# Attention into expert-choice layer on one core: ninth-block evictions one place later, finished logits on GpSimd, row transposes in eight-tile units over two pairs of banks, and the last pair's products in one run

## The chip, the core and the metric

The program runs on one core of a Trainium2 chip. The core has TensorE (matrix products and transposes, PE in the rows; its weight loads are PEld), VectorE (DVE), ScalarE (ACT), GpSimd (POOL) and SyncE, whose queue issues most transfers (SPq). Each engine works through its own list in order; semaphores hold an instruction back until what it needs is there. PSUM, where TensorE writes, has eight banks of 128 x 512 floats. The metric is device time of one execution, in microseconds (us).

## The reference, cut to what matters

```
scores = q @ k^T / 8                       # 8 batches x 8 heads, 576 x 576, head size 64
keep   = scores >= max(row) - tau          # tau = 0.02
attn   = exp(scores - max), dropped entries 0, divided by the row sum
x      = (attn @ v), heads side by side    # 4608 tokens x 512
logits = x @ w_gate                        # 8 experts
# all 36864 logits in falling order: a token goes to the expert of its highest
# logit that still has room; an expert takes 576 tokens
out[token] = relu(x[token] @ w1[e]) @ w2[e]   # 512 -> 1024 -> 512
```

## The kernel before, in words

**Attention.** Two heads make a pair: 32 pairs, four per batch. A row tile is 128 queries by 576 keys, laid out as 128 x 2 x 288 in a pair of PSUM banks, a tile `sc` (there are two such pairs, for two heads). A pair has four and a half tiles per head, so two pairs together make nine units: a *cycle* `c` is nine passes of the loop over `s_` (I call a pass a *slot*; unit `u=s_%9`; `u==4` is the tile shared by both pairs, 64 queries of each). There are 16 cycles; two cycles are a batch.

In a slot the work of three units overlaps. `score` writes two `sc` tiles on TensorE. `mx` has VectorE copy each into SBUF as `z`, scaled, with the row minimum (`z` L87); GpSimd adds the threshold (`nb` L88); ScalarE takes the exponential (`ex`, `pp` L95); VectorE drops what is below the threshold and sums (`stt`, `pp` L98). Then TensorE transposes `pp` in blocks of 64 keys: eight of the nine blocks go into one PSUM pair `tb` (`tr`, L108), which ScalarE evicts into `pt` (`trev`, L120 for `u==4`, L123 for others). The *ninth blocks* of one or two units have no room there and are put into the spare columns (288 and up) of the second `sc` tile of the next slot (`left`, at `u` in 1, 3, 4, 6, 8); `leftev` evicts them (L136, L139). `columns` multiplies the finished `pt` by `v` (`group`, L154), accumulating over nine blocks `k` in the PSUM pair `vb`, by a table `plan` of which blocks of which pair go in which slot; `shut` (L158) evicts the sum into `xt`, the batch's transposed output.

**Logits of a batch.** After its last pair, `finish(b)` queues two steps, which run at `s_%9==5`, one per cycle. In a cycle of even number `lg_unit` (L177) multiplies `xt` by `w_gate` into `vb`, evicted as `lt`. In the next, of odd number, `lgt_unit` transposes `lt` back into `vb`, and `lgt_ev` (L195 to L200) multiplies by the reciprocal row sums and adds over the heads on VectorE, into `Lg`.

**Rows.** The experts gather token rows, so `xt` is transposed into row form and written to DRAM (`xrows`). Batches 0 and 1 do so within the loop (`rows_turn`, `rows_ev`: four 128-wide transposes in spare columns of the slot's two `sc` tiles, at `s_%9` in 3, 6, 8). The other six do so after the loop in 30 late units (`late_unit`; four transposes L221, or two L217 for the last 64 queries of a batch) through the two halves of `vb`. ScalarE evicts each (L223, L219). `rows_out` issues one 260 KB transfer per 128 rows; `short_out` (L209) issues 16 of 8 KB for the short tile.

**Router and experts.** `R.phase` searches, for one expert at a time, for the logit that 576 tokens reach: seven rounds of a comparison on VectorE (`cmp`), a count on TensorE (L457, L463, L479) and a step. For the first expert these rounds are interleaved with the late units by planned costs: each late unit is put down at `XTY` = 1.05 us, each round by its VectorE work. Then come the final threshold (`lo`), the expert's number (`e`), the token numbers (`idx`), the gather (L723), and the first product of the expert layer (L804). From there two lines of products, L804 and L836, run to the end; later experts' searches lie beneath them.

Of the kernel before, what the change touches and what calls it, by code (L numbers as in the profile page):

```python
# [18 lines left out]
S=576; D=64; HS=288; QK=2*HS+2*S; NB=9; XE=8*HS+256  # L19
PPB=8; LTB=1; VTB=4; HOLD=1; XW=520; NBO=2; NDEF=4; XTB=4; XTY=1.05; XT0=2.0; XRB=2  # L20


# [943 lines left out]
```

## Time and profile before

| | |
|---|---|
| median of 3 runs | 1026.44 us (1025.98 to 1026.49) |
| profiled execution | 1027.05 us |
| its span, first to last instruction | 1025.3 us |
| TensorE, VectorE, ScalarE, GpSimd busy | 93%, 75%, 61%, 22% |
| attention loop up to the first late unit | 0 to 467.7 us |
| late units and first search | 467.7 to 513.2 us |
| up to the first product of the expert layer | 545.6 us |
| expert layer | 545.6 to 1025.3 us |

The profiled execution's own time is 1.75 us longer than its span. The shares are averages over stages with different limits, so the stages are read one by one. TensorE's granted clock is a share of its full 2.4 GHz; 0.50 is 1.2 GHz.

### The profile page before, as it was taken

How to read it: one execution, taken by the hardware profiler on the slowest of the kernel's cores; microseconds unless marked ns; L12 is line 12 of the kernel's file. 1: busy time of each engine (PE TensorE's matmuls, PEld its weight loads, DVE VectorE, ACT ScalarE, POOL GpSimd, SP SyncE). 2: the span in 40 equal slices, each digit the busy share in tenths (PEclk: the TensorE clock that was granted, in tenths of full speed). 3: DMA queues.
4: the chain of work that ended last, by engine and by line, in shares of the span. 5: the costliest groups of instructions: out<-in, count | busy, mean ns of one | idle time of the engine just before them, and what ended most of it. 6: DMA issues, size and time to landing. Idle time of an engine off the chain costs nothing.

```text
span 1025.3 us, 25919 instructions
## 1 busy us (share of the span) xinstructions
PE 956.2 (93%) x10337; PEld 727.7 (71%) x10337; DVE 770.3 (75%) x2100; ACT 621.1 (61%) x1059; POOL 229.8 (22%) x308
## 2 busy tenths in 40 slices
PE   7999999999999999996737999999999999999996
PEld 4666666666666565664537879798897989899895
DVE  7999999999999999982237988868678787625230
ACT  6888898989889898963315435344342544535340
POOL 2222222324222322210010040313222213220201
PEclk9999999999999999997567999999999999999999
DMA  5222232523322230205244252534343416252101
GB/s 195 83 93 83 73 135 90 183 68 103 137 93 84 76 107 20 94 2 193 98 142 163 94 161 93 155 109 145 119 130 104 142 55 187 81 168 68 42 11 41
DMA packets 44312, 108.16 MB, mean 105 GB/s; under 512 B 13344, under 2 KB 14112, under 8 KB 43680
## 3 DMA queue, kind: packets, MB, share of 16 engines
q1 hardware_dynamic: 36800, 83.89, 24.2%
q0 software_dynamic: 5888, 19.03, 6.0%
q10 hardware_dynamic: 1504, 3.59, 1.1%
q8 instruction: 81, 1.33, 0.5%
q14 instruction: 39, 0.32, 0.1%
HBM read 83.77 MB, written 21.64 MB: 103 GB/s over the span
## 4 chain that ended last, share of the span: by engine, by line
PE 71%; DVE 10%; ACT 8%; issue 6%; DMA 2%; SPq 2%; ACTq 0%; POOLq 0%; POOL 0%; DVEq 0%
PE pf L804 21%; PE pf L836 19%; PE vb L154 10%; PE sc L79 8%; PE tb L108 5%; DVE pp L98 4%; DVE z L87 4%; ACT pp L95 3%; PE vb L221 2%; PE pt L749 2%; SPq L209 1%; ACT pp L223 1%; ACT xt L158 1%; PE rps L457 1%; ACT pt L120 1%
## 5 line engine op out<-in xcount | busy, mean ns | idle before, releaser
L95 ACT ACTIVATE pp<-z,nb 128x576 f32<-128x576 f32 x288 | 216.3, 776 | 50.7 <-DVE z L87 48.6
L87 DVE TENSOR_SCALAR_CACHE_REDUCE z<-sc 128x576 f32<-128x576 f32 x288 | 209.9, 750 | 23.2 <-ACT pt L139 9.8
L98 DVE SCALAR_TENSOR_TENSOR pp<-z,nb,pp 128x576 f32<-128x576 f32 x288 | 223.3, 811 | 0.1
L836 PE MATMUL pf<-w2h,H 128*128 128x512 f32 x576 | 195.6, 402 | 0.5 <-DVE H L385 0.5
L79 PE MATMUL sc<-qk 64*128 64x288 f32 (+1 forms) x1280 | 177.1, 425 | 3.5 <-ACT xr L270 2.0
L88 POOL TENSOR_SCALAR nb<-nb,taub 128x2 f32<-128x2 f32 x144 | 107.7, 748 | 309.3 <-DVE z L87 201.0
L154 PE MATMUL vb<-pt,vt 64*64 64x288 f32 (+2 forms) x2336 | 170.8, 410 | 6.4 <-DVE lwm L199 2.4
L108 PEld LDWEIGHTS tb<-ident,pp 64*128 64x128 f32 x2304 | 83.7, 139 | 71.3 <-issue 37.7
L123 ACT ACTIVATE pt<-tb 128x1024 f32<-128x1024 f32 x128 | 129.2, 1010 | 3.5 <-PE tb L108 2.4
L836 PE MATMUL pf<-w2l,H 128*128 128x512 f32 x320 | 128.4, 401 | 0.0
L154 PEld LDWEIGHTS vb<-pt,vt 64*64 64x64 f32 x2336 | 78.2, 132 | 61.8 <-issue 10.4
L836 PEld LDWEIGHTS pf<-w2h,H 128*128 128x128 f32 x576 | 106.9, 189 | 19.6 <-DVE H L385 0.9
L843 POOL DMA_INDIRECT out_dram<-y,idx x40 | 46.5, 1163 | 314.2 <-ACT y L839 203.9
L79 PEld LDWEIGHTS sc<-qk 64*128 64x128 f32 (+1 forms) x1280 | 97.1, 180 | 27.1 <-DVE z L87 7.7
L108 PE MATMUL tb<-ident,pp 64*128 64x64 f32 x2304 | 103.2, 230 | 10.3 <-ACT pt L120 4.3
L804 PE MATMUL pf<-xh,w1h 128*128 128x288 f32 (+2 forms) x512 | 110.6, 302 | 0.7 <-ACT xh L750 0.7
L804 PE MATMUL pf<-xl,w1h 128*128 128x288 f32 (+2 forms) x512 | 110.0, 301 | 0.0
L804 PE MATMUL pf<-xh,w1l 128*128 128x288 f32 (+2 forms) x512 | 110.0, 301 | 0.0
L839 ACT ACTIVATE y<-pf 128x512 f32<-128x512 f32 x40 | 23.9, 597 | 125.9 <-PE pf L836 119.5
L816 ACT ACTIVATE hf<-pf 128x576 f32<-128x576 f32 x56 | 36.5, 651 | 90.0 <-PE pf L804 83.4
L804 PEld LDWEIGHTS pf<-xh,w1h 128*128 128x128 f32 x512 | 82.1, 190 | 1.6 <-ACT xh L750 1.1
L804 PEld LDWEIGHTS pf<-xl,w1h 128*128 128x128 f32 x512 | 82.1, 190 | 0.1
(187 smaller groups left out, 1193.6 us busy)
## 6 DMA issues: line engine op xcount, KB each, us to landing
qk<-qk_dram SPq DMA_DIRECT2D x31, 864.0 KB, 5.5
w2s<-w_dram SPq DMA_DIRECT2D x32, 512.0 KB, 4.9
w1s<-w_dram SPq DMA_DIRECT2D x28, 512.0 KB, 5.9
vt<-vl_dram SPq DMA_DIRECT2D x32, 288.0 KB, 4.8
xrows<-pp SPq DMA_DIRECT2D x24, 260.0 KB, 2.6
xts<-xt SPq DMA_DIRECT2D x2, 1280.0 KB, 5.9
pt<-xts SPq DMA_DIRECT2D x2, 1280.0 KB, 7.1
xrows<-xr SPq DMA_DIRECT2D x8, 260.0 KB, 2.6
```

Source lines behind the costliest of these rows:

```text
L79: T.matmul(sc[o,f,:HS], LD[p]["q",h][r,q], LD[p]["k",h][r,:],start=True,stop=True)
L87: V.tensor_scalar(z,SC.pop(t)[:,:,:HS],-0.125,None,op0=ALU.mult,op1=ALU.min,accum_out=nb[:,0,t%2:t%2+1])
L88: G.tensor_scalar(nb[:,1],nb[:,0],taub[:,0:1],None,op0=ALU.add)
L95: A.activation(pview(t),zview(t),AF.Exp,bias=NBI[t][:,0:1],scale=-1.0)
L98: V.scalar_tensor_tensor(pv,zview(t),NBI[t][:,1:2],pv,op0=ALU.is_le,op1=ALU.mult,accum_out=den_of(t//36)[:,n:n+1])
L108: g=slice(64*r,64*r+64); T.transpose(o[:,r],x[g],ident[g,g])
L123: A.activation(pt_of(p)[:,0:8,o:o+128].rearrange("p k (r q) -> p r k q",r=2),tb,AF.Copy)
L154: T.matmul(vb[64*f:64*f+64,h,a:e],v[g,64*k:64*k+64],pt[g,k,HS*f+a:HS*f+e],start=(k==0 and x!=(160,HS)),stop=(k==8),skip_group_check=True)
L804: T.matmul(ps[:,h,:n],s[w][:,k,f*128:(f+1)*128],s[x][:,k,cols[h]],start=(i==0),stop=(i==11))
L816: A.activation(hf,ps[:,:,:HS],AF.Relu)
L836: T.matmul(ps[:,0,:],H[:,f,c:c+128],s[w][:,f],start=(f==0 and j==0),stop=e)
L843: G.indirect_dma_start(out=out,out_offset=IOA(ap=s["idx"][:n,t:t+1],axis=0),in_=y[:n],in_offset=None)
```

## The change

1. `leftev` is called behind the slot's first `ex` and ahead of `rows_ev` and the second `ex`; before, it was called ahead of `mx`. The ninth block of the shared tile (`u==4`) is transposed three slots later (`SL=3`), at `s_%9==8`.
2. The finished logits of batches 0 to 5 are copied from `vb` by ScalarE (two instructions) and multiplied and added by GpSimd (six instructions): `lgt_copy`. Batches 6 and 7 keep `lgt_ev`.
3. The copy of the 64 short columns into a block of its own (`xs`, GpSimd, L240 and L332) is gone; the short rows come straight out of `xt` with 32 columns at a time, and `short_out` issues 2 transfers of 64 KB in place of 16 of 8 KB. Rows within the loop are six units per batch (five before), at `s_%9` in 3 and 6.
4. `late_unit`: 18 units of eight transposes instead of 30, by turns in a fresh `tb` and a fresh `vb` pair, each evicted by one ScalarE instruction of 128 x 1024 (32 x 1024 for short tiles), with `XTY` = 1.35.
5. The last pair's nine blocks run together after the loop into an `sc` pair, behind `shut` of the pair before; its logits are one run, and one eviction.
6. In `group` and `lg_unit` the order of products within a block changes: half `h` outside, `f` (or `j`) inside.

```diff
-S=576; D=64; HS=288; QK=2*HS+2*S; NB=9; XE=8*HS+256
+S=576; D=64; HS=288; QK=2*HS+2*S; NB=9; SL=3; XE=8*HS
-PPB=8; LTB=1; VTB=4; HOLD=1; XW=520; NBO=2; NDEF=4; XTB=4; XTY=1.05; XT0=2.0; XRB=2
+PPB=8; LTB=1; VTB=4; HOLD=1; XW=520; NBO=2; NDEF=4; XTB=4; XTY=1.35; XT0=2.0; XRB=2
...
-    def left(s_,t):
+    def left(s_,t,only=None):
         c,u=divmod(s_,9)
-        if u not in (1,3,4,6,8): return
+        if u not in (1,3,6,8) and u!=only or s_<0: return
...
-    def group(p,k,f0=(0,HS),f1=(0,HS)):
-        v=LD[p]["v"]; pt=PT[p]
-        for f,x in enumerate((f0,f1)):
-            if not x: continue
-            a,e=x
-            for h in range(2):
+    def group(p,k,to=None):
+        v=LD[p]["v"]; pt=PT[p]; to=vb if to is None else to
+        for h in range(2):
+            for f in range(2):
                 g=slice(64*h,64*h+64)
-                T.matmul(vb[64*f:64*f+64,h,a:e],v[g,64*k:64*k+64],pt[g,k,HS*f+a:HS*f+e],start=(k==0 and x!=(160,HS)),stop=(k==8),skip_group_check=True)
+                T.matmul(to[64*f:64*f+64,h,:HS],v[g,64*k:64*k+64],pt[g,k,HS*f:HS*f+HS],start=(k==0),stop=(k==8),skip_group_check=True)
...
-    def lg_unit(b,f,ps):
+    def lg_unit(b,f,ps,hs=(0,1)):
         g=slice(64*f,64*f+64)
-        for j in range(4):
-            for h in range(2):
+        for h in hs:
+            for j in range(4):
...
+    def lgt_copy(b,ps):
+        w=wk.tile([128,5,8,8],F32,name="lw",bufs=2); x=w.rearrange("p c (r j h) e -> p r c j (h e)",r=2,j=2)
+        for r in range(2): A.activation(x[:,r],lv_of(ps)[:,r],AF.Copy)
+        rd=RD[b]
+        G.tensor_tensor(w[:,0:4],w[:,0:4],rd[:,0:32].rearrange("p (c x) -> p c x",c=4).unsqueeze(3).to_broadcast([128,4,8,8]),op=ALU.mult)
+        G.tensor_tensor(w[:,4],w[:,4],rd[:,36:44].unsqueeze(2).to_broadcast([128,8,8]),op=ALU.mult)
+        for n in (4,2): G.tensor_tensor(w[:,:,0:n],w[:,:,0:n],w[:,:,n:2*n],op=ALU.add)
+        g=slice(64*(b%2),64*(b%2)+64)
+        G.tensor_tensor(Lg[:,4*b:4*b+4,:],w[:,0:4,0],w[:,0:4,1],op=ALU.add)
+        G.tensor_tensor(Lg[g,32+b//2,:],w[g,4,0],w[g,4,1],op=ALU.add)
...
-    def short_out(b,x):
-        for n in range(2):
-            for f in range(2):
-                d=xrows[b*S+512+32*f:b*S+544+32*f,256*n:256*n+256].rearrange("q (x d) -> x q d",x=4)
-                for y in range(4): nc.sync.dma_start(d[y],x[32*y:32*y+32,n,f])
+    def short_out(b,xr):
+        for f in range(2): nc.sync.dma_start(xrows[b*S+512+32*f:b*S+544+32*f,0:512],xr[0:32,f])
...
-    def late_unit(b,qb,n,k):
-        ps=vb[:,k%2].rearrange("p (x f d) -> p x f d",x=4,f=2); pf=vb[:,k%2].rearrange("p (x e) -> p x e",x=4)
...
+    def late_unit(b,qb,k):
+        ps=(ps_v.tile([128,2,512],F32,name="vb") if k%2 else ps_t.tile([128,2,512],F32,name="tb")).rearrange("p a b -> p (a b)")
+        n=32 if qb==2 else 128; o=32+128*qb if qb<2 else 0
+        for i in range(8): T.transpose(ps[:n,128*i:128*i+128],xh(b)[:,i,o:o+n],ident)
+        xr=wk.tile([128,NB,2,64],F32,name="pp",bufs=PPB).rearrange("p k h d -> p (k h d)")[:,:2*XW].rearrange("p (f x) -> p f x",f=2)
+        A.activation(xr[:n,:,:512].rearrange("p f (x d) -> p f x d",x=8),ps[:n].rearrange("p (x f d) -> p f x d",x=8,f=2),AF.Copy)
+        if qb==2: short_out(b,xr[:,:,:512]); return
+        A.activation(xr[:,:,512:XW],fac(b,qb),AF.Copy); rows_out(b,qb,xr)
...
     def finish(b):
-        m=xs(b).rearrange("p (x q) -> p x q",x=8)
-        G.tensor_scalar(m,xh(b)[:,:,0:32],1.0,0.0,op0=ALU.mult,op1=ALU.add)
...
         if ev_: left(s_-1,sc_[-1] if sc_ else None)
+        if (s_-5)%9==SL: left(s_-1-SL,sc_[-1] if sc_ else None,4)
...
-        rt=bool(rows) and sc_ and s_%9 in (3,6,8)
+        rt=bool(rows) and sc_ and s_%9 in (3,6)
...
-            trev(s_-1); leftev(s_-1)
+            trev(s_-1)
...
         for t in sc_[:1]: ex(t)
+        if gate and gate[1] and s_<z-2: lgt_copy(gate[0],gp)
+        leftev(s_-1); leftev(s_-1-SL)
         if rt: rows_ev()
         for t in sc_[1:]: ex(t)
-        if gate and gate[1]: lgt_ev(gate[0],gp)
+        if gate and gate[1] and s_==z-2: lgt_ev(gate[0],gp)
...
         if s_==z-1:
-            for k in range(9): group(NP-1,k,(0,HS),(0,160) if k<8 else None)
+            for k in (7,8): group(NP-2,k)
+            pend.append(lambda: shut(NP-2))
...
-    lo,hi=slice(0,64),slice(64,128)
-    for k in range(9): group(p,k,None,(160 if k<8 else 0,HS))
     gp=ps_s.tile([128,2,512],F32,name="sc")
-    shut(p,lo); lg_unit(b,0,gp)
-    shut(p,hi); lg_unit(b,1,gp); ltev(b,(0,),gp); ltev(b,(1,),gp)
+    for k in range(9): group(p,k,gp)
+    for h in range(2): A.activation(xm(b)[:,p%4,h],gp[:,h,:HS],AF.Copy)
+    gp=ps_s.tile([128,2,512],F32,name="sc")
+    for h in range(2):
+        for f in range(2): lg_unit(b,f,gp,(h,))
+    ltev(b,(0,1),gp)
```

What the instruction lists show of it, at three places (the waits in brackets are on other engines' semaphores).

ScalarE in two slots of the loop, of before (L123 is `trev`, L139 `leftev`, L95 `ex`):

```order
L123 ACTIVATE pt<-tb 128x2x8x64 [waits PE_49]
L139 ACTIVATE pt<-sc 128x2x2x64 [waits PE_49]
L95 ACTIVATE pp<-z,nb 128x9x64 [waits DVE_49] x2
L123 ACTIVATE pt<-tb 128x2x8x64 [waits PE_49]
L95 ACTIVATE pp<-z,nb 128x9x64 [waits DVE_49] x2
```

and two slots after the change (L155 is `shut`):

```order
L123 ACTIVATE pt<-tb 128x2x8x64 [waits PE_49]
L95 ACTIVATE pp<-z,nb 128x9x64 [waits DVE_49]
L139 ACTIVATE pt<-sc 128x2x2x64 [waits DVE_49]
L95 ACTIVATE pp<-z,nb 128x9x64
L155 ACTIVATE xt<-vb 128x576 [waits PE_49]
```

The ninth-block eviction L139 has moved from ahead of the slot's two exponentials to between them; it waited for TensorE, and now waits for VectorE's reading of the same `sc` tile.

VectorE in the slot of an odd cycle that finishes a batch's logits, of before:

```order
L87 TENSOR_SCALAR z,nb<-sc 128x576 [waits DVE_49,PE_49]
L87 TENSOR_SCALAR z,nb<-sc 128x576 [waits DVE_49,PE_49,Activation_49]
L195 TENSOR_TENSOR lw<-vb,rd 128x4x32 [waits PE_49]
L195 TENSOR_TENSOR lw<-vb,rd 128x4x32
L196 TENSOR_REDUCE Lg<-lw 128x32 [waits DVE_49]
L199 TENSOR_TENSOR lwm<-vb,rm 64x64 [waits DMAHW5_49]
L200 TENSOR_REDUCE Lg<-lwm 64x8 [waits DVE_49]
L98 SCALAR_TENSOR_TENSOR pp,den<-z,nb,pp 128x9x64 [waits Pool_49]
```

and GpSimd there, after:

```order
L88 TENSOR_SCALAR nb<-nb,taub 128x2 [waits DVE_49,Activation_49,Pool_49] x2
L202 TENSOR_TENSOR lw<-lw,rd 128x256 [waits Activation_49]
L203 TENSOR_TENSOR lw<-lw,rd 128x64 [waits DMAHW7_49,DMAHW6_49]
L204 TENSOR_TENSOR lw<-lw 128x5x32 [waits Pool_49]
L204 TENSOR_TENSOR lw<-lw 128x5x16 [waits Pool_49]
L206 TENSOR_TENSOR Lg<-lw 128x32 [waits Pool_49]
L207 TENSOR_TENSOR Lg<-lw 64x8
L88 TENSOR_SCALAR nb<-nb,taub 128x2 [waits DVE_49] x2
```

The five VectorE instructions between a slot's `z` and its masking are gone; six GpSimd instructions stand between two thresholds `nb`.

TensorE at the first late units, of before:

```order
L221 MATMUL vb<-ident,xt 128x128 x4
L221 MATMUL vb<-ident,xt 128x128 [waits Activation_49]
L221 MATMUL vb<-ident,xt 128x128 x3
L221 MATMUL vb<-ident,xt 128x128 [waits Activation_49]
L221 MATMUL vb<-ident,xt 128x128 x3
```

and after:

```order
L218 MATMUL tb<-ident,xt 128x128 x8
L218 MATMUL vb<-ident,xt 128x128 x8
L218 MATMUL tb<-ident,xt 32x128 [waits Activation_49]
L218 MATMUL tb<-ident,xt 32x128 x7
L218 MATMUL vb<-ident,xt 128x128 [waits Activation_49]
L218 MATMUL vb<-ident,xt 128x128 x7
```

Before, the second unit already waits for ScalarE; after, the third is the first to wait. Five late units stand ahead of the first count of the search (L457 before, L453 after) and 13 between the counts of its first rounds; the last two rounds stand behind the last late unit.

## Rows read from the trace of the kernel before

**Rows 1.** The page: the span, and one of the costliest groups, the attention's products with `v` (line, engine, operation, what it writes and reads, count, then busy us and mean ns of one, then idle before).

```profile
span 1025.3 us, 25919 instructions
...
L154 PE MATMUL vb<-pt,vt 64*64 64x288 f32 (+2 forms) x2336 | 170.8, 410 | 6.4 <-DVE lwm L199 2.4
```

**Rows 2.** The view by stretches, one row per cycle (z of its first slot to that of the next cycle): cycles 1, 3, 4, 5, 7, 8, 9 and 13. Columns: the stretch, its us, then busy us and number of instructions of PE, PEld, DVE, ACT and POOL, the granted clock, the share of the transfer engines, GB/s.

```profile
37.56:64.32 26.76, 26.01 (x392) 16.38 (x390) 25.84 (x75) 24.01 (x37) 7.30 (x13) 1.00 0.19 58
91.86:121.93 30.07, 28.11 (x424) 18.47 (x420) 27.61 (x80) 25.42 (x42) 7.44 (x12) 1.00 0.33 116
...
121.93:149.68 27.75, 27.54 (x434) 17.82 (x432) 26.33 (x74) 25.25 (x42) 8.50 (x16) 1.00 0.28 93
...
149.68:180.13 30.45, 28.09 (x424) 18.46 (x420) 27.90 (x80) 25.42 (x42) 7.17 (x12) 1.00 0.33 114
...
207.54:235.93 28.39, 27.37 (x410) 17.24 (x410) 27.29 (x80) 24.16 (x37) 7.88 (x9) 1.00 0.18 55
235.93:263.11 27.18, 26.46 (x412) 16.62 (x406) 26.14 (x74) 24.64 (x38) 9.53 (x16) 1.00 0.47 170
263.11:291.88 28.77, 27.48 (x410) 17.28 (x410) 27.57 (x80) 24.16 (x37) 6.38 (x10) 1.00 0.17 53
...
374.64:403.42 28.78, 27.50 (x410) 17.26 (x410) 27.58 (x80) 24.18 (x37) 6.38 (x10) 1.00 0.18 53
```

**Rows 3.** The timeline of an undisturbed slot of cycle 15, TensorE and one ScalarE eviction: start, us, engine, line, operation, output and input, count, and in brackets the idle time before it with what ended it.

```profile
438.95 1.19 PE L79 MATMUL sc<-qk 64*128 64x288 f32 x8
...
440.07 1.20 PE L154 MATMUL vb<-pt,vt 64*64 64x288 f32 x16
...
441.75 1.19 PE L79 MATMUL sc<-qk 64*128 64x288 f32 x8
...
442.11 1.00 ACT L123 ACTIVATE pt<-tb 128x1024 f32<-128x1024 f32 x1
```

**Rows 4.** The timeline of the slot of cycle 13 in which a batch's logits are finished.

```profile
391.58 0.48 DVE L195 TENSOR_TENSOR lw<-vb,rd 128x128 f32<-128x128 f32 x2
...
393.03 1.69 PE L154 MATMUL vb<-pt,vt 64*64 64x288 f32 x24 [0.55 <-DVE lwm L199]
393.31 0.82 DVE L98 SCALAR_TENSOR_TENSOR pp<-z,nb,pp 128x576 f32<-128x576 f32 x1
```

**Rows 5.** The view of waits within 30 to 445 us: waiting instruction, what released it, us in all, times, us of the median.

```profile
DVE z L87 <- ACT pt L139: 9.8, 28, 0.4
...
DVE z L87 <- ACT pt L136: 5.9, 14, 0.4
```

**Rows 6.** The timeline: a batch's logits product within the loop, and that of the last batch.

```profile
250.99 1.25 PE L177 MATMUL vb<-xt,wg 64*32 64x288 f32 x32
...
463.41 2.64 PE L177 MATMUL sc<-xt,wg 64*32 64x288 f32 x32
```

**Rows 7.** The timeline of late units: the first, and others at the full and at half the clock.

```profile
467.72 0.66 PE L221 MATMUL vb<-ident,xt 128*128 128x128 f32 x4
...
468.41 0.60 ACT L223 ACTIVATE pp<-vb 128x512 f32<-128x512 f32 x1 [1.55 <-PE vb L221]
...
469.06 0.66 PE L221 MATMUL vb<-ident,xt 128*128 128x128 f32 x4 [0.69 <-ACT pp L223]
...
470.31 0.21 ACT L225 ACTIVATE pp<-rd 128x16 f32<-128x16 f32 x1
...
473.21 0.44 PE L217 MATMUL vb<-ident,xt 128*128 128x128 f32 x2 [0.75 <-ACT pp L223]
...
477.49 1.11 PE L221 MATMUL vb<-ident,xt 128*128 128x128 f32 x4 [0.16 <-ACT pp L223]
...
481.15 0.69 PE L217 MATMUL vb<-ident,xt 128*128 128x128 f32 x2 [0.51 <-ACT pp L223]
```

**Rows 8.** The view by stretches, columns as in rows 2, behind the last product of the attention.

```profile
466.05:474.00 7.95, 3.91 (x28) 2.42 (x28) 3.01 (x11) 3.63 (x9) 1.11 (x5) 1.00 0.55 222
...
476.00:518.00 42.00, 29.69 (x203) 23.61 (x202) 15.14 (x52) 14.30 (x34) 0.00 (x0) 0.50 0.35 116
...
524.00:526.00 2.00, 0.68 (x13) 0.49 (x13) 0.73 (x2) 0.00 (x0) 0.00 (x0) 0.92 1.03 383
...
540.00:550.00 10.00, 6.44 (x27) 5.51 (x27) 6.25 (x17) 6.08 (x15) 0.61 (x2) 0.52 0.99 348
```

**Rows 9.** The timeline from the last comparison of the first search to the first product of the expert layer, and, from the view of the gather's line, how long its transfers took.

```profile
507.57 1.42 DVE L385 SCALAR_TENSOR_TENSOR cmp<-st,sc,b 128x1152 bf16<-128x1152 f32 x1 [1.19 <-PE sc L479]
...
513.17 0.16 DVE L385 TENSOR_TENSOR lo<-sm,sc 128x1 f32<-128x1 f32 x1 [1.96 <-PE sc L486]
...
520.93 0.17 DVE L385 SCALAR_TENSOR_TENSOR idx<-cps,ih 128x5 int32<-128x5 f32 x1
...
524.74 7.34 SPq L209 DMA_DIRECT2D xrows<-pp  x16
...
533.47 1.88 ACTq L675 DMA_DIRECT2D w1s<-w_dram  x4
...
541.99 0.69 DVE L385 TENSOR_TENSOR xg<-xg 128x512 f32<-128x512 f32 x1 [16.77 <-DMA w1s<-w_dram]
...
545.59 1.22 PE L804 MATMUL pf<-xh,w1h 128*128 128x256 f32 x4 [0.69 <-ACT xh L750]
...
DMA to landing us min/median/max: 2.9/3.7/8.3
```

More of the change, by code (lines that the diff above doesn't have):

```diff
@@ L235, in attention @@
         n=0; o=9*(p//2)+(10 if p%2 else 6)
-        for i,m in enumerate((3,2,2,2) if p<NP-2 else (3,3,3)): plan[o+i-(p==NP-2)]=[(p,x) for x in range(n,n+m)]; n+=m
+        for i,m in enumerate((3,2,2,2) if p<NP-2 else (3,3,1)): plan[o+i-(p==NP-2)]=[(p,x) for x in range(n,n+m)]; n+=m
     aux=[]; late=[]; late2=[]; st={"last":-9,"slot":0}; soon=[]; rows=[]; XN={}; pend=[]
     def finish(b):
-        m=xs(b).rearrange("p (x q) -> p x q",x=8)
-        G.tensor_scalar(m,xh(b)[:,:,0:32],1.0,0.0,op0=ALU.mult,op1=ALU.add)
         aux.extend([(b,0),(b,1)])
         if nb_batches-NDEF-NBO<=b<nb_batches-NDEF:
-            nc.sync.dma_start(xts[b],XT[b]); late2.extend(late_of(b))
-        elif b<nb_batches-NDEF: rows.extend(late_of(b))
-        else: late.extend(late_of(b))
+            nc.sync.dma_start(xts[b],XT[b]); late2.extend((b,x) for x in range(3))
+        elif b<nb_batches-NDEF: rows.extend((b,x,n) for x in range(3) for n in range(2))
+        else: late.extend((b,x) for x in range(3))
     def flush():
@@ L256, in rows_turn @@
         b,qb,n=XN["now"]=rows.pop(0)
-        if n==0: XN["xr"]=wk.tile([128,2*XW],F32,name="xr",bufs=XRB)
+        if n==0: XN["xr"]=wk.tile([128,2*XW],F32,name="xr",bufs=XRB).rearrange("p (f x) -> p f x",f=2)
         XN["sc"]=[SC[t] for t in ts]
-        for i in range(2 if qb==2 else 4):
+        m=32 if qb==2 else 128; q=32+128*qb if qb<2 else 0
+        for i in range(4):
             o=XN["sc"][i//2]; e=HS+64*(i%2)
-            turn(o[:,:,e:e+64],xs(b)[:,128*i:128*i+128] if qb==2 else xh(b)[:,4*n+i,32+128*qb:160+128*qb])
+            turn(o[:m,:,e:e+64],xh(b)[:,4*n+i,q:q+m])
     def rows_ev():
-        b,qb,n=XN.pop("now"); xr=XN["xr"]; sc=XN.pop("sc")
-        if qb==2:
-            x=xr[:,:256].rearrange("p (n f d) -> p n f d",n=2,f=2)
-            A.activation(x.rearrange("p n f d -> p f n d"),sc[0][:,:,HS:HS+128].rearrange("p f (n d) -> p f n d",n=2),AF.Copy)
-            short_out(b,x); return
-        xr=xr.rearrange("p (f x) -> p f x",f=2)
-        for k,o in enumerate(sc):
-            e=256*n+128*k; A.activation(xr[:,:,e:e+128],o[:,:,HS:HS+128],AF.Copy)
-        if n:
-            G.tensor_scalar(xr[:,:,512:XW],fac(b,qb),1.0,0.0,op0=ALU.mult,op1=ALU.add); rows_out(b,qb,xr)
+        b,qb,n=XN.pop("now"); xr=XN["xr"]; m=32 if qb==2 else 128
+        for k,o in enumerate(XN.pop("sc")):
+            e=256*n+128*k; A.activation(xr[:m,:,e:e+128],o[:m,:,HS:HS+128],AF.Copy)
+        if not n: return
+        if qb==2: short_out(b,xr[:,:,:512]); return
+        G.tensor_scalar(xr[:,:,512:XW],fac(b,qb),1.0,0.0,op0=ALU.mult,op1=ALU.add); rows_out(b,qb,xr)
     idle=cst.tile([128,128],BF16,name="idle"); V.memset(idle,0.0)
@@ L296, in attention @@
             else:
-                for f in range(2): lg_unit(gate[0],f,gp)
+                for h in range(2):
+                    for f in range(2): lg_unit(gate[0],f,gp,(h,))
                 pend.append(lambda b=gate[0]: ltev(b,(0,1),vb))
@@ L323, in attention @@
     for g in soon: g()
-    lo,hi=slice(0,64),slice(64,128)
-    for k in range(9): group(p,k,None,(160 if k<8 else 0,HS))
     gp=ps_s.tile([128,2,512],F32,name="sc")
-    shut(p,lo); lg_unit(b,0,gp)
-    shut(p,hi); lg_unit(b,1,gp); ltev(b,(0,),gp); ltev(b,(1,),gp)
+    for k in range(9): group(p,k,gp)
+    for h in range(2): A.activation(xm(b)[:,p%4,h],gp[:,h,:HS],AF.Copy)
+    gp=ps_s.tile([128,2,512],F32,name="sc")
+    for h in range(2):
+        for f in range(2): lg_unit(b,f,gp,(h,))
+    ltev(b,(0,1),gp)
     gp=ps_s.tile([128,2,512],F32,name="sc")
     lgt_unit(b,gp); lgt_ev(b,gp)
-    m=xs(b).rearrange("p (x q) -> p x q",x=8)
-    G.tensor_scalar(m,xh(b)[:,:,0:32],1.0,0.0,op0=ALU.mult,op1=ALU.add)
-    late.extend(late_of(b))
+    late.extend((b,x) for x in range(3))
     for k in range(0,NBO,2):
```

43 lines of the change are left out of this document (14 added, 29 removed).

## The prediction, written before the changed kernel ran

> **What bounds the kernel now.** I read the page first, then the view by stretches, one row per cycle, then timelines where cycles differ, and last the stretch between the attention and the expert layer. The span is 1025.3 us [rows 1]; the profiled execution took 1027.05, so 1.75 lie around the span, and the sums below are made against 1027.05, 0.6 above the median 1026.44. A difference under 0.2% (2 us) I call no change, about what a measurement of this kernel can tell.
>
> Inside the attention, cycles are not equal [rows 2]. Cycle 8, which multiplies logits but finishes none, lasts 27.18, with TensorE busy 26.46: TensorE sets it. A quiet slot shows the same, since the next scores start 2.80 us after the last (438.95 to 441.75) [rows 3], and nine of them are 25.2. The cycles that finish logits last 28.39 (7), 28.77 (9) and 28.78 (13), about 28.65, with the same instructions on TensorE. Where the excess sits is seen in one slot: five VectorE instructions occupy 391.58 to 393.31, so the mask is 1.73 late, and TensorE waits 0.55 for the last of them to free `vb` [rows 4]. The waits say the rest: VectorE's `z` waits 9.8 us for the eviction L139 and 5.9 for L136, 42 times in all, about 0.4 each [rows 5]. Cycles 3 and 5, with three row units each besides, last 30.07 and 30.45; cycle 4, with two row units and no finish, 27.75.
>
> Behind the attention nothing is TensorE-bound. The late units run 467.72 to about 513: a unit's four transposes take 0.66, its eviction 0.60, and the next transposes start only behind the eviction (469.06, 0.69 idle behind ACT) [rows 7]. At 476 to 518 the clock is 0.50 (1.2 GHz) [rows 8]. From `lo` at 513.17 the first expert's numbers take until 520.93, but its first product starts at 545.59, 32.4 us behind `lo` [rows 9].
>
> **The change, part by part.**
>
> *Finished logits.* In cycles 7, 9, 11 and 13, VectorE loses 1.73 us of work per finish, and `z` its waits on L139 and L136. What is left is cycle 8's work or cycle 1's (26.76). I take 26.9, so 4 x (28.6 - 26.9) = 6.8. Cover: ScalarE takes two copies instead, and is busy 24.2 of 28.8. GpSimd is busy 6 to 8 of a cycle; its six instructions are not in the trace, and I take 2 us for them, inside the 2.80 until the next threshold is due. If they took 3.5, 0.7 would show six times, 4 us.
>
> *Evictions L139 and L136* now wait for `z` instead. Queued behind one is the second exponential (0.4 later); the masking that needs it is a slot later. The eviction also frees the `sc` pair later, by about 0.55 after `z`; the score that wants it comes 0.6 after that by the quiet slot's spacing. So I cost this at nothing, with TensorE's own list as its cover, and say 0.4 x 28 = 11 us would be lost if that slack is not there. Nor do I add a gain in even cycles, since TensorE already fills them.
>
> *Rows in the loop.* A unit costs (27.75 - 27.18)/2 = 0.28 in an even cycle and (30.26 - 28.65)/3 = 0.54 in an odd one. Now two units in each of cycles 3 to 8. Cycles 3 and 5 go from 60.52 together to 2 x (26.9 + 1.1) = 56.0, a gain of 4.5; cycles 7 and 8, which had none, lose 1.1 and 0.6.
>
> Attention: 6.8 + 4.5 - 1.7 = 9.6, say **10**. Lower bound 4 (half the finish gain, rows as costed); upper 16 (odd cycles at TensorE's 26.46, row units free).
>
> *The last pair.* Its logits went in halves, 2.64; the same 32 records in one run are 1.25 [rows 6]: 1.4. Its blocks now wait for the evictions of the pair before, about 0.3. Gain **1.1**.
>
> *Late units and search.* Eight transposes cost TensorE 0.88 at full clock: two more transposes cost 0.66 - 0.44 = 0.22, so 0.11 each; at half clock (1.11 - 0.69)/2 = 0.21 [rows 7]. ScalarE: 1.00 for 128 x 1024 [rows 3] and 0.21 for the factors [rows 7], so 18 x 1.00 + 12 x 0.21 = 20.5, against 18 x 0.88 = 15.8 on TensorE. With two pairs of banks the two overlap, so ScalarE sets it: 20.5 at least. Counts of the search stand in TensorE's list between them and wait for VectorE; I add 4 and get 24.5 (bounds 20.5 and 30). Then the last two rounds run without company. A round ends with its comparison, 1.42; the last before, from its comparison to `lo`, took 5.6 with units between at half clock [rows 9]; I take 3 each. So 24.5 + 6 = 30.5 against 513.17 - 467.72 = 45.45: a gain of **15**.
>
> *From `lo` to the first product.* Before, `idx` comes 7.9 behind `lo`, then weights are asked for at 533.47 and gathered rows are first used at 541.99, though a gather lands in 3.7. What is late are row transfers: L209's 16 small ones occupied SyncE's queue for 7.34 us from 524.74 [rows 9]; both gather and weight load stand behind the last of them. With 6 transfers per batch instead of 20, and units done earlier by two rounds of the search, that backlog is gone before `lo`. Left: 7.9, then 4.1 for issue and landing, then 3.6 (541.99 to 545.59): 15.7 instead of 32.4, a gain of **16.7**. The weights, asked for at `e`, are to land beneath the 12 us before that use.
>
> *No cost or gain:* the removed short-column copies (GpSimd is idle there), and the order within a block of products, as long as TensorE overlaps its quarter-size products as before: 2336 records of 410 ns lie in 170.8 busy us [rows 1], so over five are in flight. From 545.59 on, the expert layer is the same: its 479.7 stay, give or take 2, since its first 4 us ran at half clock [rows 8] and may not now.
>
> Sum: 10 + 1.1 + 15 + 16.7 = 42.8; 1027.05 - 42.8 = **984**.
>
> **The clock.** The trace leaves one thing open. For 8 us behind the last product, transposes alone kept the clock at 1.00 although TensorE was busy 3.91 of 7.95; then it fell, and stayed at 0.50 for 42 us with TensorE busy 29.69 of them, transposes mostly [rows 8]. After the change TensorE is busy over 80% of the late units (15.8 + 4 of 24.5), denser than either; I lean to full clock. If transposes do not keep it, eight cost 1.70 instead of 0.88. The Trainium skill ("TensorE: Matmul & The Clock Gate", Part 4: PE-mode transpose) says that the full rate does not engage for transposes, as they do not count as busy the same way. By that rule the half-clock case below holds; the 42 us at 0.50 agree with it, the 8 us at 1.00 do not.
>
> **The rivals.**
>
> 1. *Half clock in the late units.* The first five units run before the clock falls; 13 then cost 1.70 - 0.88 = 0.82 more and TensorE becomes their bound: 10.7 us, so **995**. For it, the 42 us above; against it, the 8.
>
> 2. *The attention gains little.* A slot's chain of `z`, exponential, mask and transposes has its own length, and the later L139 or GpSimd's chain may take the place of what is removed: 4 instead of 10, **990**. For it: TensorE is within 1.3 us of cycle 9's span already (27.48 of 28.77), partly by stretched records.
>
> 3. *The first product does not come earlier.* If gather and weights still wait for the last row transfers, or the rows' transfers pile up because units come faster, `idx` to first use stays long: 12.4 of the 16.7 are given back (521.1 to 533.47), **997**. Against it: 36 transfers instead of 120 through the queue.
>
> 4. *Slower.* The order within a block puts two products on the same rows of the array next to each other, and a block's four products might overlap less. The products with `v` are 170.8 us busy [rows 1], 16 records in 1.20 [rows 3], on the engine that sets the attention. A quarter more is 43 us and eats all gains; half more gives 984 + 85 = **1069**; from there on it decides against the rest. Against it: the logits' records already run many on the same row half at a time, 32 in 1.25 [rows 6].
>
> **Numbers.** Full clock and the sum as it stands 0.52; half clock 0.30; little from the attention 0.10; the late first product 0.06; slower 0.02. The likeliest gives 984. The range reaches from 974 (attention 16, late units at ScalarE's 20.5) to 1002, which takes in half clock with a small attention gain (995 + 6). The likeliest alone would be 976 to 991. Each case but the fourth is faster by far more than 0.2%: 0.97 faster, 0.01 the same, 0.02 slower.
>
> **What would show it.** Cycles 7, 9, 11 and 13 near 26.9, and no wait of `z` on L139 or L136; if cycles stay above 28, the second rival. Products with `v` at 1.20 per 16 records; if more, the fourth. Late units every 1.2 to 1.4 us with clock 1.00; if 1.7 to 1.9 with 0.50, the first. `idx` to the first use of gathered rows near 4; if over 10, the third. I am wrong most easily in adding separately three gains that share one queue of transfers: units that come faster ask SyncE for 260 KB per 1.4 us.

## The result: 981.63 us, 4.4% faster

The changed kernel takes 981.63 us (980.03 to 982.50, 4 runs) against 1026.47 before on the same chip: a ratio of 0.9556, 95% interval 0.9535 to 0.9578. The prediction said 984, range 974 to 1002. The profiled execution took 980.79 with a span of 979.1.

The page, and the products with `v` (compare [rows 1]):

```profile
span 979.1 us, 25952 instructions
...
L151 PE MATMUL vb<-pt,vt 64*64 64x288 f32 x2232 | 164.9, 416 | 0.3 <-ACT pt L120 0.3
```

The view by stretches, cycles 3, 7, 8, 9, 13 and 14, columns as in [rows 2]:

```profile
90.57:118.10 27.53, 27.04 (x414) 17.77 (x412) 26.12 (x74) 25.07 (x43) 10.61 (x17) 1.00 0.22 75
...
201.02:228.51 27.49, 27.00 (x414) 17.65 (x412) 26.11 (x74) 25.05 (x43) 10.58 (x17) 1.00 0.24 76
228.51:255.98 27.47, 27.42 (x428) 17.34 (x426) 26.18 (x75) 24.71 (x40) 7.44 (x14) 1.00 0.48 168
255.98:282.66 26.68, 26.23 (x398) 16.87 (x396) 26.11 (x74) 24.17 (x39) 10.01 (x16) 1.00 0.19 57
...
363.30:389.98 26.68, 26.23 (x398) 16.86 (x396) 26.11 (x75) 24.18 (x39) 10.00 (x16) 1.00 0.19 58
389.98:416.96 26.98, 26.98 (x420) 16.97 (x418) 26.22 (x75) 24.34 (x38) 7.44 (x14) 1.00 0.26 90
```

Cycles 9 and 13 went from 28.77 and 28.78 to 26.68; cycle 8 rose from 27.18 to 27.47, since it now carries two row units.

The timeline of the end of the attention (compare [rows 6] for the logits' product):

```profile
442.07 0.94 PE L108 MATMUL tb<-ident,pp 64*128 64x64 f32 x16 [1.77 <-DVE pp L98]
...
442.94 2.20 PE L151 MATMUL vb<-pt,vt 64*64 64x288 f32 x16
...
446.82 4.59 PE L151 MATMUL sc<-pt,vt 64*64 64x288 f32 x70 [0.53 <-ACT pt L123]
...
451.34 1.78 PE L174 MATMUL sc<-xt,wg 64*32 64x288 f32 x32
...
454.76 1.09 PE L218 MATMUL tb<-ident,xt 128*128 128x128 f32 x8
```

The view by stretches there:

```profile
443.00:444.00 1.00, 1.00 (x13) 0.53 (x16) 0.96 (x3) 0.00 (x0) 0.00 (x0) 0.50 0.00 0
444.00:445.00 1.00, 1.00 (x12) 0.20 (x4) 1.00 (x2) 0.00 (x0) 0.00 (x0) 0.50 0.08 16
```

TensorE is idle for 1.77 us, and the 16 records behind take 2.20 instead of 1.20, at a granted clock of 0.50.

The late units by stretches (compare [rows 8]), then the timeline to the first expert product (compare [rows 9]):

```profile
454.76:478.85 24.09, 20.50 (x228) 17.72 (x226) 12.87 (x43) 18.99 (x30) 0.00 (x0) 1.00 0.76 270
478.85:487.00 8.15, 3.63 (x43) 3.08 (x44) 5.31 (x21) 0.00 (x1) 0.00 (x0) 0.56 0.32 106
```

```profile
483.05 0.16 DVE L381 TENSOR_TENSOR lo<-sm,rps 128x1 f32<-128x1 f32 x1 [0.57 <-PE rps L482]
...
485.38 1.89 ACTq L671 DMA_DIRECT2D w1s<-w_dram  x4
...
490.51 0.17 DVE L381 SCALAR_TENSOR_TENSOR idx<-cps,ih 128x5 int32<-128x5 f32 x1
...
495.56 0.69 DVE L381 TENSOR_TENSOR xg<-xg 128x512 f32<-128x512 f32 x1 [0.77 <-DMA xg<-xrows,idx]
...
500.00 1.22 PE L800 MATMUL pf<-xh,w1h 128*128 128x256 f32 x4 [0.69 <-ACT xh L746]
```

Where the 46.2 us of span went, from these starts and those of before:

| stage | before | after | gain | predicted |
|---|---|---|---|---|
| start to cycle 0 | 12.05 | 11.33 | 0.7 | 0 |
| cycles 0 to 14 | 418.56 | 405.63 | 12.9 | 10 |
| cycle 15 to the first late unit | 37.11 | 37.80 | -0.7 | 1.1 |
| first late unit to `lo` | 45.45 | 28.29 | 17.2 | 15 |
| `lo` to the first expert product | 32.42 | 16.95 | 15.5 | 16.7 |
| expert layer | 479.71 | 479.10 | 0.6 | 0 |

The 0.7 at the start is not the change's: cycle 0 starts anywhere from 10.6 to 12.3 us in the profiles of the changed kernel and its variants below.

### The profile page after: what moved, and what is told of

It reads as the page before. It is cut to its first block, busy times and chain, and to the rows that moved or that the text cites. A ratio compares the mean times of both kernels' runs of the same rounds, so it can differ in the third digit from the quotient of the medians.

```text
span 979.1 us, 25952 instructions
## 1 busy us (share of the span) xinstructions
PE 939.3 (96%) x10365; PEld 718.5 (73%) x10365; DVE 761.3 (78%) x2070; ACT 620.2 (63%) x1064; POOL 241.3 (25%) x334
## 4 chain that ended last, share of the span: by engine, by line
PE 83%; ACT 6%; DVE 5%; issue 2%; DMA 2%; POOL 0%; POOLq 0%; ACTq 0%; SPq 0%; DVEq 0%
PE pf L800 21%; PE pf L832 20%; PE vb L151 13%; PE sc L79 12%; PE tb L108 8%; ACT pp L95 3%; PE pt L745 2%; DVE pp L98 1%; PE sc L108 1%; PE rps L453 1%; DVE z L87 1%; ACT pt L123 1%; ACT pt L120 1%; DMA out_dram<-y,idx 1%; PE vb L174 1%
## 5 line engine op out<-in xcount | busy, mean ns | idle before, releaser
L95 ACT ACTIVATE pp<-z,nb 128x576 f32<-128x576 f32 x288 | 218.4, 777 | 39.9 <-DVE z L87 39.1
L87 DVE TENSOR_SCALAR_CACHE_REDUCE z<-sc 128x576 f32<-128x576 f32 x288 | 206.6, 752 | 18.7 <-PE sc L79 11.8
L79 PE MATMUL sc<-qk 64*128 64x288 f32 (+1 forms) x1280 | 173.5, 419 | 3.1 <-DMA qk<-qk_dram 1.9
L88 POOL TENSOR_SCALAR nb<-nb,taub 128x2 f32<-128x2 f32 x144 | 99.0, 687 | 284.2 <-ACT pp L95 180.3
L151 PE MATMUL vb<-pt,vt 64*64 64x288 f32 x2232 | 164.9, 416 | 0.3 <-ACT pt L120 0.3
L123 ACT ACTIVATE pt<-tb 128x1024 f32<-128x1024 f32 x128 | 131.0, 1023 | 8.3 <-PE tb L108 7.8
L151 PEld LDWEIGHTS vb<-pt,vt 64*64 64x64 f32 x2232 | 73.5, 133 | 50.7 <-issue 8.8
```

Source lines behind the costliest of these rows:

```text
L79: T.matmul(sc[o,f,:HS], LD[p]["q",h][r,q], LD[p]["k",h][r,:],start=True,stop=True)
L87: V.tensor_scalar(z,SC.pop(t)[:,:,:HS],-0.125,None,op0=ALU.mult,op1=ALU.min,accum_out=nb[:,0,t%2:t%2+1])
L88: G.tensor_scalar(nb[:,1],nb[:,0],taub[:,0:1],None,op0=ALU.add)
L95: A.activation(pview(t),zview(t),AF.Exp,bias=NBI[t][:,0:1],scale=-1.0)
L123: A.activation(pt_of(p)[:,0:8,o:o+128].rearrange("p k (r q) -> p r k q",r=2),tb,AF.Copy)
L151: T.matmul(to[64*f:64*f+64,h,:HS],v[g,64*k:64*k+64],pt[g,k,HS*f:HS*f+HS],start=(k==0),stop=(k==8),skip_group_check=True)
```

## The experiments

All change the changed kernel. The runs from the old order of products on, and the one on the shared tile's ninth block, were on two other chips, where the expert layer is longer for every kernel (482.8 to 491.6 us; the kernel before took 1033.14 and 1036.60 there). So ratios to the kernel before on the same chip are given, and otherwise stages are compared; times that an expectation names for these runs go by the first chip.

**Finished logits back on VectorE.**

```diff
-        if gate and gate[1] and s_<z-2: lgt_copy(gate[0],gp)
...
-        if gate and gate[1] and s_==z-2: lgt_ev(gate[0],gp)
+        if gate and gate[1]: lgt_ev(gate[0],gp)
```

> The changed kernel with the finished logits of all batches back on VectorE (lgt_ev behind the second exponential), everything else as changed. If VectorE's 1.7 us in the finishing slot is what made the odd cycles long, the six finishing cycles are about 1.7 us longer again (cycles 9, 11 and 13 at 28.3 to 28.7 instead of 26.68), about 10 us: 991 to 993. Rival: the later ninth-block eviction is what shortened them; then at most 3 us: 982 to 985.

Measured 988.60, ratio 0.9632 (0.9612 to 0.9652). By stretches, cycles 9 and 13:

```profile
259.11:287.42 28.31, 27.55 (x408) 17.18 (x408) 27.58 (x80) 23.80 (x37) 6.30 (x10) 1.00 0.17 54
...
368.95:397.26 28.31, 27.56 (x408) 17.18 (x408) 27.58 (x80) 23.80 (x37) 6.30 (x10) 1.00 0.17 54
```

The two go from 26.68 to 28.31, 1.63 each, close to the 1.73 of VectorE's work in [rows 4]; cycles 0 to 14 grow by 7.1 in all, not 10, as cycles 3, 5, 7 and 11 lose 0.9 to 1.3 only and cycles 10, 12 and 14 are 0.2 shorter. So the time stays below the 991 to 993 expected. TensorE's wait for `vb`, which [rows 4] shows too, is not what costs the 1.63. The timeline of the finishing slot of cycle 13 in this run:

```profile
386.58 0.23 DVE L196 TENSOR_TENSOR lw<-vb,rd 64x64 f32<-64x64 f32 x1
...
386.93 1.69 PE L151 MATMUL vb<-pt,vt 64*64 64x288 f32 x24
...
388.86 0.71 PE L108 MATMUL tb<-ident,pp 64*128 64x64 f32 x16 [0.24 <-DVE pp L98]
```

The products into `vb` start with no idle time of TensorE in front of them; it is the masking that comes late. This edit is over half of the attention's gain.

**Ninth-block evictions first again.**

```diff
-            trev(s_-1)
+            trev(s_-1); leftev(s_-1); leftev(s_-1-SL)
...
-        leftev(s_-1); leftev(s_-1-SL)
```

> The changed kernel with leftev ahead of the slot's row minima again, everything else as changed. My working put this edit at nothing: 981 to 984. Rival: the waits of z on L139 and L136 (15.7 us in the kernel before) come back as time on the path, about 0.5 us per cycle: 988 to 991, and z waits for L139 and L136 stand in the view of waits again.

Measured 983.46, ratio 0.9578 (0.9561 to 0.9595). The view of waits within 30 to 430 us (us in all, times, the longest; in [rows 5], too, the last column is the longest and not the median):

```profile
DVE z L87 <- ACT pt L139: 10.9, 32, 0.4
```

Of the 15.7 us of waits in [rows 5], 10.9 are back, 0.34 each on the mean, and cycles 0 to 14 take only 1.3 more, nearly all of it in cycles 3 to 8, which carry rows. A short wait on an engine that has slack is hardly any time, so costing the move at nothing was close; removing these waits is what the view seemed to promise, and it is not where the gain came from.

**The shared tile's ninth block one slot behind its tile** (on the last-pair kernel, below).

```diff
-        if u not in ((1,3,6,8) if c<z//9-1 else (1,3,4,6,8)) and u!=only or s_<0: return
+        if u not in (1,3,4,6,8) and u!=only or s_<0: return
...
-        if (s_-5)%9==SL and s_<z-1: left(s_-1-SL,sc_[-1] if sc_ else None,4)
```

> The last-pair experiment with the shared tile's ninth block transposed one slot behind its tile in every cycle, as before the change, instead of four. If that deferral is what makes the cycles without a finish 0.2 to 0.3 us shorter than before, cycles 1, 2, 10, 12 and 14 go back to 26.76, 27.54 and 27.18, about 3 us over the attention. Rival: the deferral moves the eviction from one slot to another and the cycles stay within 0.1 us.

Ratio 0.9558 (0.9524 to 0.9592). The result lies between the two: cycles 3, 5, 7, 9, 11 and 13, which finish logits, are 0.24 longer than in the last-pair kernel, 8 by 0.17, 10, 12 and 14 by 0.07, 1 and 2 not at all; 1.85 us over cycles 0 to 14. So the deferral helps the finishing cycles, and hardly those that the theory named. If they add, the three experiments give back 10.3 of 12.9. The rest, the rows in two slots of nine and what the edits do to each other, was not tried apart; why cycles 1, 2, 10, 12 and 14 are 0.2 to 0.3 shorter than before stays open, but for the 0.07.

**Short rows in 16 transfers.**

```diff
-        for f in range(2): nc.sync.dma_start(xrows[b*S+512+32*f:b*S+544+32*f,0:512],xr[0:32,f])
+        for f in range(2):
+            for y in range(8): nc.sync.dma_start(xrows[b*S+512+32*f:b*S+544+32*f,64*y:64*y+64],xr[0:32,f,64*y:64*y+64])
```

> The changed kernel with the short rows written in 16 transfers of 8 KB instead of 2 of 64 KB, everything else as changed. SyncE needed 61.5 us for the 120 row transfers of the six late batches in the kernel before (470.54 to 532). If that queue is the bound, the row transfers run from 457 to about 519 here, and the first expert product comes near 532 instead of 500.0: about 32 us more, 1010 to 1016, so that the faster late units are worth nothing without this edit. Rival: units that finish earlier are enough, the 12.4 us of the third rival at most: 982 to 994.

Measured 1012.93, ratio 0.9875 (0.9850 to 0.9901). The timeline of SyncE's queue, its first and last batch, and of ScalarE's and GpSimd's, then ScalarE's longest wait among the late units:

```profile
457.15 1.84 SPq L211 DMA_DIRECT2D xrows<-pp  x4
459.21 7.53 SPq L214 DMA_DIRECT2D xrows<-pp  x16
...
508.45 1.81 SPq L211 DMA_DIRECT2D xrows<-pp  x4
510.36 7.65 SPq L214 DMA_DIRECT2D xrows<-pp  x16
...
519.40 1.89 ACTq L672 DMA_DIRECT2D w1s<-w_dram  x4
...
520.16 1.21 POOL L720 DMA_INDIRECT xg<-xrows,idx  x1 [65.55 <-issue]
```

```profile
479.41 1.02 ACT L221 ACTIVATE pp<-vb 128x1024 f32<-128x1024 f32 x1 [7.06 <-DMA xrows<-pp]
```

An 8 KB transfer holds the queue for 0.47 us, as long as one of 260 KB (1.84 for four). The 120 row transfers last from 457 to 518, and weights and gather start only behind the last. The late units stand behind the queue as well, since ScalarE waits for transfers to free the row buffers: `lo` comes 36.05 us behind the first late unit instead of 28.29. First late unit to first expert product is 76.0, against 77.9 before and 45.2 changed: without this edit 30.8 of that stretch's 32.6 are gone.

**All late units in one pair of banks.**

```diff
-        ps=(ps_v.tile([128,2,512],F32,name="vb") if k%2 else ps_t.tile([128,2,512],F32,name="tb")).rearrange("p a b -> p (a b)")
+        ps=ps_v.tile([128,2,512],F32,name="vb").rearrange("p a b -> p (a b)")
```

> The changed kernel with all 18 late units in the one pair of banks vb, so that a unit's transposes wait for the eviction of the unit before; everything else as changed. A unit then takes 0.88 + 1.0 and two handovers, 2.1 to 2.2 instead of 1.34: 18 units 38 to 40 us instead of 24.1, so 14 to 16 us more, 995 to 998, if the clock stays at 1.00. If transposes that keep TensorE about half busy lose the clock, as behind 474 us in the kernel before, TensorE's part grows by 0.82 a unit and the time is 1003 to 1010 with granted clock 0.50 there. Rival: eight transposes per unit are the whole gain and the second pair is worth little: under 986.

Measured 1008.88, ratio 0.9837 (0.9804 to 0.9869). By stretches from the first late unit to `lo`, then the timeline of one unit at either clock:

```profile
452.84:462.00 9.16, 4.71 (x37) 3.65 (x36) 3.01 (x11) 4.40 (x7) 0.00 (x0) 1.00 0.53 200
462.00:466.00 4.00, 3.11 (x29) 2.17 (x27) 0.57 (x5) 1.38 (x3) 0.00 (x0) 0.69 0.67 255
466.00:507.60 41.60, 27.71 (x191) 23.01 (x192) 11.22 (x35) 13.84 (x21) 0.00 (x0) 0.50 0.34 120
```

```profile
455.05 1.09 PE L218 MATMUL vb<-ident,xt 128*128 128x128 f32 x8 [1.11 <-ACT pp L220]
...
479.15 1.97 PE L218 MATMUL vb<-ident,xt 128*128 128x128 f32 x8 [0.92 <-ACT pp L220]
```

Both things happened: units wait 1.1 us for the eviction before them, and the clock falls some 10 us in and stays at 0.50, as before the change. First late unit to `lo` is 54.8 instead of 28.3. The second pair pays twice: it overlaps the engines, and TensorE, busy 20.50 of 24.09, keeps its clock.

**The old order of products in a block.**

```diff
-        for h in range(2):
-            for f in range(2):
+        for f in range(2):
+            for h in range(2):
                 g=slice(64*h,64*h+64)
```

> The changed kernel with the order of products in a block as before: f outside, half h inside, in the products with v and in the logits. The sum put this at nothing: 980 to 984, products with v at 1.20 us per 16 records. The fourth rival's mechanism would show as a faster kernel here: if neighbours on the same rows overlapped less, 16 records would take clearly under 1.20.

Ratio 0.9533 (0.9501 to 0.9565). The timeline of a slot:

```profile
424.81 1.20 PE L151 MATMUL vb<-pt,vt 64*64 64x288 f32 x16
```

1.20, and cycles equal within 0.02: the fourth rival, which priced the products with `v`, is out. The edit changes these alone; the logits' products keep the new order here, so theirs was not tried. In this run the gap at the end of the attention is there but the clock stays at 1.00, and the last `z` to the first late unit takes 17.82 instead of 19.05. So the fall of the clock at 443 is not certain to follow the gap.

**The last pair but one back in its slot.**

```diff
-        if u not in (1,3,6,8) and u!=only or s_<0: return
+        if u not in ((1,3,6,8) if c<z//9-1 else (1,3,4,6,8)) and u!=only or s_<0: return
...
-        if (s_-5)%9==SL: left(s_-1-SL,sc_[-1] if sc_ else None,4)
+        if (s_-5)%9==SL and s_<z-1: left(s_-1-SL,sc_[-1] if sc_ else None,4)
...
-        for i,m in enumerate((3,2,2,2) if p<NP-2 else (3,3,1)): plan[o+i-(p==NP-2)]=[(p,x) for x in range(n,n+m)]; n+=m
+        for i,m in enumerate((3,2,2,2) if p<NP-2 else (3,3,3)): plan[o+i-(p==NP-2)]=[(p,x) for x in range(n,n+m)]; n+=m
...
-        if s_==z-1:
-            for k in (7,8): group(NP-2,k)
-            pend.append(lambda: shut(NP-2))
```

> The changed kernel with blocks 7 and 8 of the last pair but one back in the slot before (the shared tile's ninth block of the last cycle is transposed one slot after its tile, as before), the last pair's products still in one run. In the changed kernel TensorE idles from 440.3 to 442.0 and the clock is 0.50 at 443 to 445. Theory: the moved blocks opened that gap; with them in it the clock stays at 1.00, and 1.0 us of products at half speed and the wait for them go: 2 to 3 us faster than the changed kernel, 978.5 to 980. Rival: the gap is set by VectorE's masking alone and the end of the attention moves by under 0.7 us: 981 to 982.5.

Ratio 0.9515 (0.9482 to 0.9547). The timeline:

```profile
439.57 1.69 PE L151 MATMUL vb<-pt,vt 64*64 64x288 f32 x24
...
443.02 0.71 PE L108 MATMUL tb<-ident,pp 64*128 64x64 f32 x16 [1.12 <-DVE b L378]
...
444.85 4.59 PE L151 MATMUL sc<-pt,vt 64*64 64x288 f32 x70 [0.37 <-ACT pt L123]
```

The last `z` to the first late unit takes 16.28, against 19.05 in the changed kernel's profile and 17.84 in the later one whose clock did not fall: 1.6 us are the moved blocks themselves, 1.2 the clock. TensorE still waits 1.12 for the last masking, as it did before the change (`b` L378 starts where that masking ends). The second part of the theory is not secure: with the blocks moved, the clock fell here in four of seven profiles, and with them back in their slot still in one of six (the run with 1.80 us, below).

**Batch 6's logits on GpSimd too** (on the last-pair kernel: `lgt_copy` at `s_==z-2` as well).

> As the last-pair experiment, with the finished logits of batch 6 also by ScalarE and GpSimd, so that VectorE's masking of the last tile does not stand behind 1.5 us of logits. Theory: the last transposes wait for that masking, so 1 to 1.5 us less than the last-pair experiment: 977 to 979. Rival: ScalarE's chain (eviction of tb, then of the ninth blocks) is as late as the masking, and nothing changes.

Ratio 0.9510 (0.9479 to 0.9542). The rival holds; the stretch is 16.28 again. The last masking is done earlier, but the transposes now wait for something else:

```profile
442.18 0.71 PE L108 MATMUL tb<-ident,pp 64*128 64x64 f32 x16 [1.12 <-ACT pt L123]
```

There is one pair `tb`, and its eviction ends when the masking used to.

**Idle products.**

```diff
-                s.step_cmp(E); yield gap()
+                s.step_cmp(E)
+                if s.alone and i>4: s.warm(20)
+                yield gap()
...
-WARM=[20,4,50]
+WARM=[20,4,100]
```

> As the experiment before, with 20 idle products behind the comparison of each of the last two search rounds and 100 instead of 50 behind the first expert's numbers. Theory: the clock that falls at 480 and again at 497 in the changed kernel stays at 1.00, worth up to 1 us from the last round to idx and up to 2 us in the first products of the expert layer: 975 to 978. Rival: idle products stand in the way of counts and transposes and give back what the clock brings: no change from the experiment before.

Ratio 0.9572 (0.9546 to 0.9598): slower. The timeline of the last round:

```profile
478.49 1.28 PE L583 MATMUL rps<-trib,onesb 128*128 128x128 bf16 x20 [1.51 <-DVE cmp L377]
479.61 0.38 PE L449 MATMUL rps<-oh,cmp 128*128 128x32 bf16 x9
```

They did not run beneath the comparison but behind it, ahead of the count, and from the first late unit to `lo` it now takes 29.61 instead of 28.29. Up to the first expert product 1.7 us are lost. The rest of the 6.3 us between the medians lies in the expert layer (485.4 us in this profile, 483.0 in that of the experiment before), and why stays open. So the rival is right that idle products stand in the way, but the cost is more than the nothing that it gave.

**The changed kernel again, and the planner's step.** Late units put down at 1.65 and 1.80 us instead of 1.35, on the last-pair kernel (`XTY`).

> The changed kernel, unaltered, beside the two that follow on the same chip: the same stages as in its first profile, first expert product 83 us behind the start of cycle 15, and the same ratio to the kernel before.

> The last-pair experiment with late units put down at 1.65 us instead of 1.35, so that each round of the search stands earlier among them and none is left behind the last unit (two before, of which 4.2 us lay behind the last transposes). Theory: late units end as before, 24 us, and lo follows within 2 us: 2 to 3 us less than the last-pair experiment, 4.5 to 6 us less than the changed kernel on this chip (0.5% to 0.6%). Rival: counts that wait for VectorE now hold back the units behind them, the units end 2 to 3 us later and nothing is won beyond the last-pair experiment's 2.9 us.

> The same with 1.80 us: the search ends ahead of the last unit. Theory: lo another 0 to 1 us earlier, but the last rows are written behind the token numbers' start; as the gather comes 7.5 us behind lo and a row transfer lands in 2.6, that stays hidden: within 1 us of the run with 1.65. Rival: the search is held up by units in TensorE's list and lo is later than with 1.65 by 1 us or more.

On one chip: the changed kernel 989.22, ratio 0.9537 (0.9507 to 0.9566); 1.65: 985.00, 0.9494 (0.9465 to 0.9523); 1.80: 988.60, 0.9518 (0.9489 to 0.9548). In the changed kernel's profile the clock did not fall at the end of the attention this time, and its first expert product comes 81.81 behind the start of cycle 15, not 83.05. With 1.65, first late unit to `lo` is 27.50 instead of 28.29: 0.8, not 2 to 3. By stretches:

```profile
451.61:479.11 27.50, 21.76 (x255) 18.80 (x254) 14.84 (x49) 18.72 (x30) 0.00 (x0) 1.00 0.79 290
```

No round is left behind the units, but units now wait behind counts, so most of it is given back, as the rival said. With 1.80 the stretch is 28.24, but this profile says little of the planner's step, as its clock fell twice: at the end of the attention, where the last pair's 70 records took 6.16 instead of 4.59, and within the late units. By stretches, from the first late unit to `lo`:

```profile
453.82:461.20 7.38, 5.81 (x61) 4.86 (x60) 4.90 (x19) 5.17 (x8) 0.00 (x0) 1.00 0.78 293
461.30:464.60 3.30, 3.04 (x25) 2.53 (x22) 1.07 (x7) 1.16 (x3) 0.00 (x0) 0.50 0.53 202
464.70:482.06 17.36, 13.52 (x167) 11.49 (x166) 8.78 (x23) 10.86 (x18) 0.00 (x0) 1.00 0.65 229
```

So whether 1.80 is worse than 1.65 is not shown. The 1.65 version is the fastest of all by its ratio; its interval overlaps that of the changed kernel, and by stages (start of cycle 15 to the first expert product 79.46 instead of 81.81) it is 2.4 us better, 1.6 of them by the last pair's blocks. On the three chips the cycles agree within 0.02; what differs is the expert layer.

## Why the prediction held, step by step

**Attention, 10 predicted, 12.9 measured.** The four finishing cycles 7, 9, 11 and 13 gave 6.8, the figure of the term, but cycle 7 now carries two row units, which the sum took off apart; without them the four would give about 7.6 (cycle 7 lasts 27.49 and cycle 9 26.68, so two units cost 0.8 in an odd cycle, 0.4 each and not 0.54). The rows term was too careful, too: cycles 3 and 5 gained 5.5, not 4.5. And cycles 1, 2, 10, 12 and 14, put at nothing, gained 0.2 to 0.3. "TensorE already fills them" was the slip: cycle 8 of before had 0.7 us of slack, in two waits for ScalarE, and cycle 14 has none after the change (26.98 busy of 26.98). The timeline of cycle 8 of before:

```profile
238.75 1.44 PE L154 MATMUL vb<-pt,vt 64*64 64x288 f32 x20 [0.46 <-ACT xt L158]
...
254.17 1.69 PE L154 MATMUL vb<-pt,vt 64*64 64x288 f32 x24 [0.27 <-ACT lt L183]
```

The lower bound of 4 is mis-added: half the finish gain with rows as costed is 3.4 + 4.5 - 1.7 = 6.2. GpSimd's chain is mis-sized: 3.9 us instead of 2. The timeline of the finishing slot of cycle 13, and of the next slot's first masking:

```profile
380.71 1.10 POOL L202 TENSOR_TENSOR lw<-lw,rd 128x256 f32<-128x256 f32 x1
...
384.44 0.20 POOL L207 TENSOR_TENSOR Lg<-lw 64x8 f32<-64x8 f32 x1
...
384.74 0.29 POOL L88 TENSOR_SCALAR nb<-nb,taub 128x2 f32<-128x2 f32 x1
...
385.56 0.81 DVE L98 SCALAR_TENSOR_TENSOR pp<-z,nb,pp 128x576 f32<-128x576 f32 x1
```

My working said that at 3.5 it would cost 4 us. It costs nothing here: the masking uses the threshold a slot after its `z`, so it is due at 385.56, not at the end of its own slot.

**The last pair, +1.1 predicted, -0.7 measured.** I priced the logits' run (1.25 taken, 1.78 measured, since its halves still wait for two evictions) and a wait of 0.3. I did not ask what the moved blocks had covered: before, 24 records of products ran at 452.16, while the last tiles are masked; of them only 8 are left at 438.77, and TensorE stands idle. The timelines, of before and after:

```profile
452.16 1.69 PE L154 MATMUL vb<-pt,vt 64*64 64x288 f32 x24
```

```profile
438.77 0.72 PE L151 MATMUL vb<-pt,vt 64*64 64x288 f32 x8
```

The sign is that of one execution: in the later profile of the changed kernel, where the clock stayed at 1.00, this stage took 36.59 us, a gain of 0.5. The last-pair experiment puts the blocks back and takes 35.03, a gain of 2.1: they cost 1.6 whether the clock falls or not.

**Late units and search, 15 predicted, 17.2 measured.** 18 units in 24.1 us, predicted 24.5, at full clock. The lone rounds cost 4.2, not 6, as one of the two still lay beside the last units.

**`lo` to the first product, 16.7 predicted, 15.5 measured.** `idx` comes 7.46 behind `lo` (7.76 before by the same measure; the prediction's 7.9 runs to its end, and its three terms add up to 15.6, not 15.7); 5.05 to the first use of gathered rows instead of 4.1; then 4.44 instead of 3.6, with the clock down again. The third rival's price was mis-sized: not 12.4 but 31 us hang on the two transfers, because faster units alone do not shorten the queue and have to wait for it themselves.

**The clock.** The page's rule (the Trainium skill, "TensorE: Matmul & The Clock Gate", Part 4: PE-mode transpose) is not borne out: 24.09 us of transposes with the search's counts between them ran at 1.00; and in the run with 1.80 us, where the clock fell within the late units, it was back at 1.00 from 464.7, with only such transposes and counts on TensorE since its fall. The same transposes spread thinner (4.71 busy of 9.16 in one pair of banks) lost the clock, and did not get it back at 27.71 busy of 41.60. Whether transposes with no count among them would hold it for as long, no run here shows.

**The total.** It came within 3.4 us (46.2 against 42.8) in part by luck: the last pair and the first product were credited with 3.0 too much, attention and late units with 5.1 too little, and 1.3 lie in the start and the expert layer, which were put at nothing.

## What to carry to other kernels

Three stages in a row can hang on one queue: count a queue's transfers, not their bytes, before crediting a faster producer. A wait that the profile lists is worth its time only where the waiting engine sets the pace; 10.9 us of such waits came back for 1.3. Before moving work to the end to make one long run, look at which idle stretch it was filling, for the gap can cost the clock as well.
